# Ordering TensorE's work by tile shape, with two PSUM banks instead of three for transposes and attention outputs

## The chip, the cores and the metric

The kernel runs on one core of a Trainium2 chip. The metric is device time in microseconds (us) for one execution. The kernel before was run three times: 494.48, 492.61 and 491.35 us, median 492.61. One execution was also profiled, and all rows in this document come from such profiles. Engines are named as in the profile: PE is TensorE, DVE is VectorE, ACT is ScalarE, POOL is GpSimd, SP issues DMAs.

## The reference

Two stages over 8 batches of 576 positions. Stage 1 is window attention with 8 heads of 64 columns; its output, heads side by side, is the input x of stage 2, a mixture of four attention experts of which each position uses two.

```python
# stage 1, per batch and head
scores = (q @ k.T) / 8;  mask = (0 <= row - col < 64)
attn = softmax(where(mask, scores, -1e9));  y = attn @ v
# stage 2, per batch, x is (576, 512)
logits = x @ w_gate                  # 4 experts, the 2 largest are kept, softmax over them gives w
for e in range(4):
    q, k, v = x @ wq[e], x @ wk[e], x @ wv[e]
    a = softmax(causal(q @ k.T / 8))
    out += (e is chosen) * w[e] * (a @ v @ wo[e])
```

## The kernel before

**Stage 1** works in 36 units of eight (head pair, 64-row block) pieces. `s1_qk` multiplies queries by two key blocks each into two PSUM banks of the tag `s`; ACT and DVE gather the wanted half into `sm`, and the softmax follows: maximum (DVE), subtraction (POOL), exponential (ACT), sum and reciprocal (DVE), scaling (POOL). In the first five units (`u < EARLY`) the subtraction is instead the bias of eight ACT exponentials of 64 columns. `s1_t` transposes the result on PE into one bank of the tag `t`; ACT copies it (`ft`), DVE multiplies it twice by a mask straight out of the bank (`pt<-t,tri`), POOL masks the other half out of `ft`. `s1_av` multiplies by v into another `t` bank, and ACT and DVE split the result into a high and a low float32r part (`xh`, `xl`).

**Stage 2** works by batch and by pair of experts (`pr`). `s2_v`, `s2_k`, `s2_q` project x with three products each (high times high, high times low, low times high) into `s` banks. `s2_mm` makes the scores in four blocks k, two `s` banks each, and `s2_soft` their softmax in place in the tiles `p` (maxima on DVE, exponentials on ACT, and `s2_w` scales by the gate on POOL). `s2_t` transposes them into `t` banks (tiles `t2_b_pr_part_k`), ACT copies them to `pt`, `s2_av_mm` multiplies by v (`o2_b_pr_part`, tag `t`), and `s2_av_out` splits that into `yh` and `yl`. `s2_o` is the output projection: six products of 512 columns into an `s` bank (`ops`), a copy on DVE into `out`, and a DMA.

**PSUM** has eight banks: five for the tag `s`, three for `t`.

**The order** is made by the class `Plan`. Each call is only recorded, with a position `at` on a scale where one half step n is one expert pair of one batch; `Plan.order` then plays the recorded instructions on five engines with assumed lengths (`length`), assumed time to hop between engines, an assumed cost for PE when the tile shape changes (`SWITCH`), and the number of buffers per tag. Whenever an engine is free it takes the ready instruction with the lowest `place`. The result is the fixed program order of each engine. The tile shape (`mode`) of a PE instruction is the pair of rows and columns of the array that it uses: 128x128 for transposes and all projections, 64x128 for the scores of stage 2, 64x64 for the scores of stage 1, 128x64 for the products with v. All instructions of the profile carry line 241, where the recorded calls are made, so they are told apart by tile names.

Of the kernel before, what the change touches and what calls it, by code (L numbers as in the profile page):

```python
# [29 lines left out]
CPOS = 0.202  # L30
EARLY = 5
AFFINITY = 0.0
UNFOLD = (2, 2)
BPOS = ((0.044, 0.7), (0.088, 0.667), (0.08, 0.3, 0.12), (-0.413, -0.1))
# [4 lines left out]
class Plan:  # L39
# [3 lines left out]
    OVERLAP = {"V": 85, "A": 105, "G": 30, "P": 0, "S": 0}  # L43
    SWITCH = 105
    HOP = 40
# [189 lines left out]
    def place(self, op, mode):  # L235
        return op["at"] - (AFFINITY if op["mode"] == mode is not None else 0)

# [19 lines left out]
def window_attention_moe_attention(ctx: ExitStack, tc: tile.TileContext, qT, kT, vW,  # L257
# [105 lines left out]
    def s1_qk(u):  # L363

        banks = [psum.tile([128, 4, 128], F32, tag="s", bufs=5, name=f"s1_{u}_{x}") for x in range(2)]
        with nc.block():
# [36 lines left out]
    def s1_t(u):  # L403

        ps = psum.tile([128, 4, 128], F32, tag="t", bufs=3, name=f"t1_{u}")
        sm = SM.pop(u).rearrange("r x j c -> r (x j c)")
        with nc.block():
            for i in range(4):
                nc.tensor.transpose(ps[:, i], sm[:, 128 * i:128 * i + 128], ident)
        t = PT1[u] = work.tile([128, 4, 2, 128], F32, tag="pt1", bufs=2, name=f"pt1_{u}")  # L410
        f = work.tile([128, 4, 128], F32, tag="ft", bufs=1, name=f"ft_{u}")
        nc.scalar.activation(f, ps, AF.Copy)
        for e in range(2):
            r = slice(64 * e, 64 * e + 64)
            if e < UNFOLD[u >= EARLY]:
                nc.vector.tensor_mul(t[0:64, :, e], ps[r],
                                     tri[r].rearrange("r a c -> r (a c)")[:, None, :].to_broadcast([64, 4, 128]))
            for half in range(e < UNFOLD[u >= EARLY], 2):
                nc.gpsimd.affine_select(out=t[64 * half:64 * half + 64, :, e].rearrange("r i (a c) -> r i a c", a=2),
                                        in_=f[r].rearrange("r i (a c) -> r i a c", a=2), pattern=[[0, 4], [0, 2], [2 * half - 1, 64]],  # L420
                                        base=half - 1, channel_multiplier=1 - 2 * half, compare_op=OP.is_ge, fill=0.0)

    freed = []

    def s1_av(u):
        t = PT1.pop(u)
        o = psum.tile([128, 8, 64], F32, tag="t", bufs=3, name=f"o1_{u}")
        with nc.block():
# [100 lines left out]
    def s2_v(b, j):  # L529


        ps = psum.tile([128, 512], F32, tag="s", bufs=5, name=f"v2ps_{b}_{j}")
        with nc.block():
# [56 lines left out]
    def proj(b, name, pr, half):  # L590
        c0, n = HALVES[b > 0][half]
        ps = psum.tile([128, 512], F32, tag="s", bufs=5, name=f"{name}ps_{b}_{pr}_{half}")
        w = slice(128 * pr, 128 * pr + 128)
# [38 lines left out]
    def s2_mm(b, pr, k):  # L632
        banks = SB[b, pr, k] = [psum.tile([128, 512], F32, tag="s", bufs=5, name=f"s2_{b}_{pr}_{k}_{e}")
                                for e in range(2)]
# [53 lines left out]
    def s2_w(b, pr, k):  # L688
# [7 lines left out]
        for x in range(x0, x1):  # L696
            i, e = (x + 1) // 2, (x + 1) % 2
            p = PX[0][:, 0] if x == 0 else P2S[pr][i > 2][:, row(i, e):row(i, e) + 64 + 128 * i]
            nc.gpsimd.tensor_scalar(p, p, r2[:, 3, x:x + 1], 1.0, op0=OP.mult, op1=OP.mult)

    def s2_t(b, pr, part, k):
        ps = psum.tile([128, 512], F32, tag="t", bufs=3, name=f"t2_{b}_{pr}_{part}_{k}")
        pt = PT2[part]
# [43 lines left out]
        else:  # L747
# [18 lines left out]
    def s2_av_mm(b, pr, part):  # L766
        b0, b1 = PARTS[part]
        n = 64 * (b1 - b0)
        o = OB[b, pr, part] = psum.tile([128, 512], F32, tag="t", bufs=3, name=f"o2_{b}_{pr}_{part}")
        with nc.block():  # L770
# [5 lines left out]
    def s2_av_out(b, pr, part):  # L776
        b0, b1 = PARTS[part]
        o = OB.pop((b, pr, part))
        for x0, x1 in ([(b0, b1)] if b % 2 == 0 or b1 < BLK else [(b0, b1 - 1), (b1 - 1, b1)]):
            src = o[:, 64 * (x0 - b0):64 * (x1 - b0)]  # L780
            y0 = y_col(b, x0)
            yh, yl = (y[pr][:, y0:y0 + 64 * (x1 - x0)] for y in (YH, YL))
            nc.scalar.activation(yh, src, AF.Copy)
            nc.vector.tensor_sub(yl, src, yh)

    def s2_o(b, j):
        ps = psum.tile([128, DM], F32, tag="s", bufs=5, name=f"ops_{b}_{j}")
# [14 lines left out]
    def half(n):  # L802
# [10 lines left out]
        if 0 <= zb < NB and n >= 2:  # L813
# [120 lines left out]
```

## Time and profile before

| | |
|---|---|
| median of three runs | 492.61 us (491.35 to 494.48) |
| profiled execution | 494.5 us, span of its instructions 492.8 us |
| PE busy | 466.4 us, 95% of the span |
| DVE, ACT, POOL busy | 356.0, 309.5, 231.5 us (72%, 63%, 47%) |
| mean granted clock of PE | 0.985 |
| HBM | 39.85 MB read, 9.44 MB written |

How to read it: a PE row's duration runs from its start to a modelled end, and the next matmul starts before that end. So the difference between the starts of two rows is the better measure of what a block of matmuls takes on PE. Idle time of an engine is given with what released it.

### The profile page before, as it was taken

The numbers are of one execution on the slowest core, as the hardware profiler recorded it, in microseconds if no ns is written. First come the engines' busy times: TensorE is split into PE (matmuls) and PEld (weight loads), VectorE is DVE, ScalarE is ACT, GpSimd is POOL, SyncE is SP. The second block draws the span as 40 slices with busy tenths as digits, with TensorE's granted clock in tenths as the row PEclk, the third lists the DMA queues.
The fourth block names the chain that finished last, engine by engine and source line by source line (L and its number), as shares of the span: only waits on it lengthen the run. The fifth ranks groups of instructions, "written<-read, shape, count | busy, mean of one in ns | idle before, by whom it ended". The sixth has DMA issues, their size and how long they took to land.

```text
span 492.8 us, 14724 instructions
## 1 busy us (share of the span) xinstructions
PE 466.4 (95%) x5672; PEld 411.8 (84%) x5672; DVE 356.0 (72%) x1186; ACT 309.5 (63%) x967; POOL 231.5 (47%) x434
## 2 busy tenths in 40 slices
PE   5597979999999999999999999999999999999986
PEld 3487968898889988898889988898888988898774
DVE  4778987988777967687776868868776875555712
ACT  4566556767575766757567676667567575656751
POOL 3456647563555464562555544462555450512130
PEclk9979989999999999999999999999999999999989
DMA  7954742214362323223451324234120011001103
GB/s 232 386 180 152 235 145 68 81 49 120 122 187 86 107 88 99 75 94 98 140 189 51 103 86 136 77 98 125 66 92 1 2 45 40 27 1 45 43 2 108
DMA packets 21782, 50.24 MB, mean 102 GB/s; under 512 B 2896, under 2 KB 5456, under 8 KB 21712
## 3 DMA queue, kind: packets, MB, share of 16 engines
q1 hardware_dynamic: 21712, 49.30, 30.7%
q8 instruction: 45, 0.74, 0.6%
q14 instruction: 25, 0.20, 0.1%
HBM read 39.85 MB, written 9.44 MB: 100 GB/s over the span
## 4 chain that ended last, share of the span: by engine, by line
PE 86%; DVE 6%; ACT 4%; issue 1%; POOL 1%; DMA 1%; SPq 1%; POOLq 0%; ACTq 0%
PE s L241 17%; PE o L241 17%; PE t L241 13%; PE ops L241 11%; PE qps L241 10%; PE v2ps L241 10%; PE kps L241 10%; ACT sm L241 2%; DVE st L241 2%; DVE pt L241 2%; DMA k<-in_kT_dram 1%; DVE sm L241 1%; ACT p L241 1%; SPq L241 1%; DVE p L241 0%
## 5 line engine op out<-in xcount | busy, mean ns | idle before, releaser
L241 POOL TENSOR_TENSOR sm<-sm,st 128x512 f32<-128x512 f32 x67 | 71.5, 1070 | 86.4 <-DVE st L241 53.6
L241 PE MATMUL o<-pt,v 128*64 128x64 f32 (+3 forms) x2048 | 94.3, 248 | 6.7 <-DVE pt L241 3.5
L241 PEld LDWEIGHTS o<-pt,v 128*64 128x64 f32 x2048 | 84.8, 142 | 17.3 <-issue 8.3
L241 POOL TENSOR_SCALAR p<-p,r 128x192 f32<-128x192 f32 (+3 forms) x128 | 72.7, 587 | 38.7 <-DVE r L241 24.0
L241 ACT ACTIVATE p<-p,r 128x192 f32<-128x192 f32 (+3 forms) x128 | 77.6, 608 | 21.2 <-DVE r L241 21.0
L241 ACT ACTIVATE pt<-t 128x512 f32<-128x512 f32 (+2 forms) x192 | 69.8, 386 | 15.9 <-PE t L241 13.8
L241 DVE CUSTOM_DVE_ANT_0 p<-s,causal 128x320 f32<-128x320 f32 (+3 forms) x160 | 70.5, 471 | 11.5 <-PE s L241 10.3
L241 POOL TENSOR_SCALAR_AFFINE_SELECT pt<-ft 64x512 f32<-64x512 f32 x72 | 48.3, 671 | 54.8 <-ACT ft L241 50.7
L241 PE MATMUL t<-ident,p 128*128 128x128 f32 x384 | 58.5, 278 | 1.0 <-POOL p L241 0.8
L241 DVE TENSOR_REDUCE st<-sm 128x8 f32<-128x512 f32 x72 | 49.0, 681 | 9.0 <-ACT sm L241 8.1
L241 DVE TENSOR_TENSOR pt<-t,tri 64x512 f32<-64x512 f32 x72 | 49.4, 686 | 6.4 <-ACT ft L241 5.3
L241 PE MATMUL s<-kt,qt 64*128 64x256 f32 (+2 forms) x480 | 53.2, 336 | 0.4 <-DVE logits L241 0.4
L241 PEld LDWEIGHTS t<-ident,p 128*128 128x128 f32 x384 | 43.5, 142 | 9.8 <-issue 4.0
L241 PE MATMUL s<-k,q 64*64 64x128 f32 (+1 forms) x1152 | 45.4, 293 | 6.2 <-DMA k<-in_kT_dram 4.6
L241 PEld LDWEIGHTS s<-k,q 64*64 64x64 f32 x1152 | 35.5, 147 | 12.9 <-issue 4.7
L241 PEld LDWEIGHTS s<-kt,qt 64*128 64x128 f32 x480 | 34.9, 186 | 10.6 <-issue 4.1
L241 DVE COPY_PREDICATED sm<-own,s 128x256 f32<-128x256 uint8 x72 | 30.9, 444 | 14.2 <-ACT sm L241 9.7
L241 PE MATMUL qps<-xh,wqhi 128*128 128x320 f32 (+1 forms) x128 | 40.5, 316 | 0.1
L241 PE MATMUL kps<-xh,wkhi 128*128 128x320 f32 (+1 forms) x128 | 39.5, 309 | 0.0
L241 PE MATMUL v2ps<-wvhi,xh 128*128 128x260 f32 x128 | 38.7, 303 | 0.0
L241 PE MATMUL qps<-xl,wqhi 128*128 128x320 f32 (+1 forms) x128 | 37.6, 294 | 0.0
L241 PE MATMUL kps<-xh,wklo 128*128 128x320 f32 (+1 forms) x128 | 37.6, 294 | 0.0
(106 smaller groups left out, 1028.7 us busy)
## 6 DMA issues: line engine op xcount, KB each, us to landing
v<-in_vW_dram SPq DMA_DIRECT2D x32, 576.0 KB, 4.0
out_dram<-out SPq DMA_DIRECT2D x32, 256.0 KB, 2.0
q<-in_qT_dram SPq DMA_DIRECT2D x28, 288.0 KB, 3.2
k<-in_kT_dram SPq DMA_DIRECT2D x28, 288.0 KB, 4.1
out_dram<-out SPq DMA_DIRECT2D x8, 128.0 KB, 2.3
q<-in_qT_dram SPq DMA_DIRECT2D x4, 160.0 KB, 5.5
k<-in_kT_dram SPq DMA_DIRECT2D x4, 160.0 KB, 4.9
q<-in_qT_dram SPq DMA_DIRECT2D x4, 128.0 KB, 2.3
```

The costliest lines, as they stand in the source:

```text
L241: call(*args, **kw)
```

## The change

- `AFFINITY` goes from 0 to 0.6: `place` lets an instruction of PE's present tile shape come up to 0.6 of a half step before its position. It holds for positions below 15 (`2 * NB - 1`).
- `SWITCH` and several assumed lengths in `length` change (transposes, float32 and float32r products, POOL and ACT instructions).
- The tag `s` has six banks and `t` two. The transposes of the last batch take `s` banks.
- `EARLY` is gone: all 36 units subtract on POOL and use one exponential of 512 columns. `UNFOLD`, which was (2, 2), is gone; what it selected stays.
- The four output projections of batch 6 get one position, `OLATE` = 1.7 half steps after the start of their half step. So that they can still read the values of batch 6, those of batch 7 (and the last block of batch 6, which is projected with it) are put in buffers of their own, taken from the tags `xh` and `xl`.
- In the last batch the copies of the second and fourth output projection are made on ACT.

```diff
+OLATE = 1.7
+TTAG = 1
+AFFINITY = 0.6
-EARLY = 5
-AFFINITY = 0.0
-UNFOLD = (2, 2)
...
-    SWITCH = 105
+    SWITCH = 100
...
         if name == "transpose":
-            return 109
+            return 105
         if ins[0].dtype == F32R:
-            return (0.215 * n + 13) if rows == 64 else max(109, 0.43 * n + 10)
+            return (0.215 * n + 19) if rows == 64 else 0.43 * n + 14
         if rows == 64:
-            return max(28, 0.43 * n)
-        return 2 * max(28, 0.43 * n) if cols == 64 else 2 * max(110, 0.86 * n)
+            return 33 + 0.22 * n
+        return 6 + 0.86 * n if cols == 64 else 20 + 1.72 * n
...
     def place(self, op, mode):
-        return op["at"] - (AFFINITY if op["mode"] == mode is not None else 0)
+        return op["at"] - (AFFINITY if op["mode"] == mode and op["at"] < 2 * NB - 1 else 0)
...
-        if u < EARLY:
-            nc.vector.tensor_scalar(st[:, 0], st[:, 0], 0.125, None, op0=OP.mult)
-            for i in range(8):
-                nc.scalar.activation(flat[:, i], flat[:, i], AF.Exp, bias=st[:, 0, i:i + 1], scale=0.125)
-        else:
-            nc.gpsimd.tensor_tensor(flat, flat, st[:, 0, :, None].to_broadcast([128, 8, 64]), op=OP.add)
-            nc.scalar.activation(flat, flat, AF.Exp, scale=0.125)
+        nc.gpsimd.tensor_tensor(flat, flat, st[:, 0, :, None].to_broadcast([128, 8, 64]), op=OP.add)
+        nc.scalar.activation(flat, flat, AF.Exp, scale=0.125)
...
-        ps = psum.tile([128, 4, 128], F32, tag="t", bufs=3, name=f"t1_{u}")
+        ps = psum.tile([128, 4, 128], F32, tag="t", bufs=2, name=f"t1_{u}")
...
+    T2 = (dict(tag="t", bufs=2), dict(tag="s", bufs=6))
+
     def s2_t(b, pr, part, k):
-        ps = psum.tile([128, 512], F32, tag="t", bufs=3, name=f"t2_{b}_{pr}_{part}_{k}")
+        ps = psum.tile([128, 512], F32, **T2[b == NB - 1 and TTAG], name=f"t2_{b}_{pr}_{part}_{k}")
...
+    def y_buf(b, blk):
+
+        if b < NB - 2 or b == NB - 2 and blk < BLK - 1:
+            return YH, YL
+        if not Y7:
+            for x in ("xh", "xl"):
+                t = work.tile([128, NP * S], F32R, tag=x, name=f"y7{x}")
+                Y7.append([t[:, 1152 * i:1152 * i + S + 64] for i in range(2)])
+        return Y7
...
-        nc.vector.tensor_copy(t, ps)
+        if b == NB - 1 and j % 2:
+            nc.scalar.activation(t, ps, AF.Copy)
+        else:
+            nc.vector.tensor_copy(t, ps)
...
             if zp == 1:
-                spread("O0", [(s2_o, zb, j) for j in range(2)])
-                spread("O1", [(s2_o, zb, j) for j in range(2, 4 + zb % 2)])
+                if zb == NB - 2:
+                    it += [(n + OLATE, s2_o, (zb, j)) for j in range(4)]
+                else:
+                    spread("O0", [(s2_o, zb, j) for j in range(2)])
+                    spread("O1", [(s2_o, zb, j) for j in range(2, 4 + zb % 2)])
```

What this does to PE's program order, counted over its 4056 matmuls: the tile shape changes 236 times before and 157 times with the change. By the shape that is entered: 64x128 63 times before and 41 now, 128x64 51 and 45, 64x64 32 and 19, 128x128 90 and 52. From the first score block of batch 1 to that of batch 7 the counts are 167 and 91. The matmuls themselves are the same.

Three places in the order, PE alone. The first is in the middle, where batch 3 ends and batch 4 begins, from the same transpose on. Only the first row or rows of each block are shown; names are tile, then unit or batch, pair and block. Before:

```order
L241 MATMUL t2_3_1_1_2_721<-ident_86,p2_2_69 128x128 x4
L241 MATMUL s1_27_0_725<-k24_612,q24_611 64x64 x2
...
L241 MATMUL t2_3_1_1_3_722<-ident_86,p2_2_69 128x128 x4
L241 MATMUL kps_4_1_1_729<-xh4_517,wkhi_171 128x256
...
L241 MATMUL o1_26_733<-pt1_26_716,v23_620 64x64 x16
L241 MATMUL o2_3_1_1_735<-pt2_1_88,v2_1_102 64x64 x2
...
L241 MATMUL s2_4_0_2_0_736<-kt_4_0_682,qt0_91 128x320
...
L241 MATMUL s1_28_0_740<-k24_612,q24_611 64x128 x2
...
L241 MATMUL s2_4_0_3_0_738<-kt_4_0_682,qt0_91 128x256
...
L241 MATMUL t1_27_730<-ident_86,sm1_27_727 128x128 x4
```

With the change:

```order
L241 MATMUL t2_3_1_1_2_721<-ident_86,p2_2_69 128x128 x4
L241 MATMUL s1_27_0_725<-k24_612,q24_611 64x64 x2
...
L241 MATMUL s1_28_0_740<-k24_612,q24_611 64x128 x2
...
L241 MATMUL t2_3_1_1_3_722<-ident_86,p2_2_69 128x128 x4
L241 MATMUL t2_4_0_0_0_747<-ident_86,p2_0_67 128x128 x4
L241 MATMUL s2_4_0_3_0_738<-kt_4_0_682,qt0_91 128x256
...
L241 MATMUL s2_4_1_2_0_797<-kt_4_1_703,qt1_92 128x320
...
L241 MATMUL o1_26_733<-pt1_26_716,v23_620 64x64 x16
L241 MATMUL o2_3_1_1_735<-pt2_1_88,v2_1_102 64x64 x2
...
L241 MATMUL s1_29_0_777<-k25_641,q25_640 64x128 x2
...
L241 MATMUL t2_4_0_0_1_758<-ident_86,p2_0_67 128x128 x4
```

Two units of 64x64 now stand together, then two transposes, then two score blocks, then the products with v as before. In the first piece the shape changes seven times over ten blocks (a projection `kps` among them), in the second six times over eleven.

The second place is a little earlier, with the change alone. The built program puts `t1_26` and `o2_3_1_0` in the same one of the two `t` banks, so `o2_3_1_0` waits until ACT and DVE have read `t1_26`:

```order
L241 MATMUL t1_26_715<-ident_86,sm1_26_695 128x128 x4
L241 MATMUL o1_25_704<-pt1_25_684,v22_614 64x64 x14
L241 MATMUL o1_25_704<-pt1_25_684,v23_620 64x64 x2
L241 MATMUL s2_4_0_1_0_709<-kt_4_0_682,qt0_91 128x448
...
L241 MATMUL s2_4_0_2_0_736<-kt_4_0_682,qt0_91 128x320
...
L241 MATMUL o2_3_1_0_706<-pt2_0_87,v2_1_102 64x64 x2
```

Between the two stand 16 products with v and two score blocks of six.

The third is in the last batch, from the last small score product on. Before:

```order
L241 MATMUL s2_7_1_1_0_1053<-kf_7_1_1018,qf1_98 128x64
L241 MATMUL t2_7_0_1_0_1061<-ident_86,p2_1_68 128x128 x4
L241 MATMUL s2_7_1_2_0_1062<-kt_7_1_1019,qt1_92 128x320
...
L241 MATMUL s2_7_1_3_0_1064<-kt_7_1_1019,qt1_92 128x256
...
L241 MATMUL t2_7_0_1_2_1058<-ident_86,p2_1_68 128x128 x4
L241 MATMUL t2_7_1_0_2_1059<-ident_86,px_70 128x128
L241 MATMUL t2_7_0_1_1_1060<-ident_86,p2_1_68 128x128 x4
L241 MATMUL t2_7_1_0_1_1066<-ident_86,p2_0_67 128x128 x4
L241 MATMUL o2_7_0_1_1068<-pt2_1_88,v2_1_102 64x64 x2
...
L241 MATMUL t2_7_1_0_0_1067<-ident_86,p2_0_67 128x128 x4
L241 MATMUL t2_7_1_1_0_1070<-ident_86,p2_2_69 128x128 x4
```

With the change:

```order
L241 MATMUL s2_7_1_1_0_1047<-kf_7_1_1020,qf1_98 128x64
L241 MATMUL t2_7_0_1_0_1055<-ident_86,p2_1_68 128x128 x4
L241 MATMUL s2_7_1_3_0_1058<-kt_7_1_1021,qt1_92 128x256
...
L241 MATMUL ops_6_2_1070<-wohi_237,yh0_93 128x512
...
L241 MATMUL ops_6_3_1072<-wohi_237,yh0_93 128x512
...
L241 MATMUL t2_7_1_0_2_1053<-ident_86,px_70 128x128
L241 MATMUL t2_7_0_1_1_1054<-ident_86,p2_1_68 128x128 x4
L241 MATMUL t2_7_1_0_1_1060<-ident_86,p2_0_67 128x128 x4
L241 MATMUL o2_7_0_1_1062<-pt2_1_88,v2_1_102 64x64 x2
...
L241 MATMUL t2_7_1_0_0_1061<-ident_86,p2_0_67 128x128 x4
L241 MATMUL t2_7_1_1_0_1064<-ident_86,p2_2_69 128x128 x4
```

Two output projections of batch 6 now stand between the last scores and the transpose of `px`, and the score block k = 2 (`s2_7_1_2`) has gone ahead, out of this piece. In DVE's order the copies of these two projections stand between the two groups of gate scales (`r`) of the last pair.

## Rows read from the trace of the kernel before

**Rows 1.** Page, the chain that ended last: shares by engine, by tile.

```profile
PE 86%; DVE 6%; ACT 4%; issue 1%; POOL 1%; DMA 1%; SPq 1%; POOLq 0%; ACTq 0%
PE s L241 17%; PE o L241 17%; PE t L241 13%; PE ops L241 11%; PE qps L241 10%; PE v2ps L241 10%; PE kps L241 10%; ACT sm L241 2%; DVE st L241 2%; DVE pt L241 2%; DMA k<-in_kT_dram 1%; DVE sm L241 1%; ACT p L241 1%; SPq L241 1%; DVE p L241 0%
```

**Rows 2.** Busy time by stretch.

```profile
core 0: us, PE busy (x) PEld busy (x) DVE busy (x) ACT busy (x) POOL busy (x), PEclk, DMA share, GB/s
0.00:100.00 100.00, 81.35 (x1132) 70.89 (x1133) 78.91 (x235) 60.69 (x190) 56.40 (x126) 0.95 0.55 183
...
112.00:442.00 330.00, 329.62 (x4021) 293.38 (x4019) 244.97 (x845) 215.00 (x673) 158.86 (x282) 1.00 0.28 88
...
460.00:480.00 20.00, 17.33 (x161) 14.02 (x161) 8.52 (x38) 14.02 (x44) 6.31 (x11) 0.91 0.07 27
```

**Rows 3.** PE timeline: start us, duration us, engine, line, operation, tiles, shapes, count.

```profile
203.60 1.09 PE L241 MATMUL t<-ident,p 128*128 128x128 f32 x8
...
206.51 0.70 PE L241 MATMUL s<-kt,qt 64*128 64x320 f32 x6
207.15 1.09 PE L241 MATMUL s<-k,q 64*64 64x128 f32 x32
208.17 0.66 PE L241 MATMUL t<-ident,p 128*128 128x128 f32 x4
208.75 0.62 PE L241 MATMUL s<-kt,qt 64*128 64x256 f32 x6
209.30 1.15 PE L241 MATMUL o<-pt,v 128*64 128x64 f32 x32
```

**Rows 4.** PE timeline: two score blocks joined, and what follows.

```profile
461.54 1.07 PE L241 MATMUL s<-kt,qt 64*128 64x256 f32 x12
462.54 1.21 PE L241 MATMUL o<-pt,v 128*64 128x64 f32 x20
```

**Rows 5.** PE timeline: a projection between two score blocks, its first three matmuls.

```profile
255.81 0.39 PE L241 MATMUL v2ps<-wvhi,xh 128*128 128x260 f32 x1
256.04 0.28 PE L241 MATMUL v2ps<-wvlo,xh 128*128 128x260 f32 x1
256.16 0.29 PE L241 MATMUL v2ps<-wvhi,xl 128*128 128x260 f32 x1
...
257.46 0.47 PE L241 MATMUL s<-kt,qt 64*128 64x448 f32 x2
```

**Rows 6.** ACT and DVE groups that read a stage-1 transpose: count, busy us, mean ns.

```profile
L241 ACT ACTIVATE ft<-t 128x512 f32<-128x512 f32 x36 | 21.3, 592 | 3.0 <-PE t L241 2.5
...
L241 DVE TENSOR_TENSOR pt<-t,tri 64x512 f32<-64x512 f32 x72 | 49.4, 686 | 6.4 <-ACT ft L241 5.3
```

**Rows 7.** Timelines of PE and DVE: one stage-1 transpose, and its last readers.

```profile
247.58 0.66 PE L241 MATMUL t<-ident,sm 128*128 128x128 f32 x4
...
250.39 1.40 DVE L241 TENSOR_TENSOR pt<-t,tri 64x512 f32<-64x512 f32 x2
```

**Rows 8.** PE timeline after the last scores.

```profile
468.97 0.33 PE L241 MATMUL t<-ident,px 128*128 128x128 f32 x1 [1.64 <-POOL px L241]
...
471.31 3.60 PE L241 MATMUL o<-pt,v 128*64 128x64 f32 x36
474.85 0.34 PE L241 MATMUL t<-ident,p 128*128 128x128 f32 x1
```

**Rows 9.** PE timeline: the same product with v, the last of the kernel.

```profile
481.74 1.98 PE L241 MATMUL o<-pt,v 128*64 128x64 f32 x36
```

**Rows 10.** POOL timeline after the last scores.

```profile
468.95 3.06 POOL L241 TENSOR_SCALAR p<-p,r 128x192 f32<-128x192 f32 x6
472.18 1.46 POOL L241 TENSOR_SCALAR p<-p,r 128x576 f32<-128x576 f32 x2 [0.17 <-DVE r L241]
```

**Rows 11.** ACT and POOL groups of the stage-1 subtraction: count, busy us, mean ns.

```profile
L241 ACT ACTIVATE sm<-sm,st 128x64 f32<-128x64 f32 x40 | 10.2, 335 | 4.5 <-DVE st L241 4.5
...
L241 POOL TENSOR_TENSOR sm<-sm,st 128x512 f32<-128x512 f32 x67 | 71.5, 1070 | 86.4 <-DVE st L241 53.6 <-ACT pt L241 7.4 <-ACT xh L241 4.9
```

More of the change, by code (lines that the diff above doesn't have):

```diff
@@ L76, in length @@
         if engine == "A":
-            return (165 if psum else 205) + 0.83 * n + (230 if len(outs) > 1 else 0)
+            return (165 if psum else 205) + 0.83 * n + (230 if len(outs) > 1 else 75 if len(ins) > 1 else 0)
         if engine == "V":
             n = max([n] + [x.free_size() for x in ins])
-            return 152 + 1.04 * n + (65 if len(outs) > 1 else 0)
+            return 152 + 1.04 * n
         if engine == "G":
             return {"tensor_tensor": 60 + 1.97 * n, "affine_select": 190 + 0.94 * n,
-                    "memset": 100 + 0.8 * n}.get(name, 265 + 0.85 * n)
+                    "memset": 100 + 0.7 * n}.get(name, (265 if outs[0].shape[0] > 64 else 190) + 0.83 * n)
         if engine == "S":
@@ L363, in s1_qk @@
     def s1_qk(u):
-        banks = [psum.tile([128, 4, 128], F32, tag="s", bufs=5, name=f"s1_{u}_{x}") for x in range(2)]
+        banks = [psum.tile([128, 4, 128], F32, tag="s", bufs=6, name=f"s1_{u}_{x}") for x in range(2)]
         with nc.block():
@@ L414, in s1_t @@
             r = slice(64 * e, 64 * e + 64)
[L415 to L421, printed above, removed]
+            nc.vector.tensor_mul(t[0:64, :, e], ps[r],
+                                 tri[r].rearrange("r a c -> r (a c)")[:, None, :].to_broadcast([64, 4, 128]))
+            nc.gpsimd.affine_select(out=t[64:128, :, e].rearrange("r i (a c) -> r i a c", a=2),
+                                    in_=f[r].rearrange("r i (a c) -> r i a c", a=2), pattern=[[0, 4], [0, 2], [1, 64]],
+                                    base=0, channel_multiplier=-1, compare_op=OP.is_ge, fill=0.0)
     freed = []
@@ L426, in s1_av @@
         t = PT1.pop(u)
-        o = psum.tile([128, 8, 64], F32, tag="t", bufs=3, name=f"o1_{u}")
+        o = psum.tile([128, 8, 64], F32, tag="t", bufs=2, name=f"o1_{u}")
         with nc.block():
@@ L529, in s2_v @@
     def s2_v(b, j):
-        ps = psum.tile([128, 512], F32, tag="s", bufs=5, name=f"v2ps_{b}_{j}")
+        ps = psum.tile([128, 512], F32, tag="s", bufs=6, name=f"v2ps_{b}_{j}")
         with nc.block():
@@ L591, in proj @@
         c0, n = HALVES[b > 0][half]
-        ps = psum.tile([128, 512], F32, tag="s", bufs=5, name=f"{name}ps_{b}_{pr}_{half}")
+        ps = psum.tile([128, 512], F32, tag="s", bufs=6, name=f"{name}ps_{b}_{pr}_{half}")
         w = slice(128 * pr, 128 * pr + 128)
@@ L632, in s2_mm @@
     def s2_mm(b, pr, k):
-        banks = SB[b, pr, k] = [psum.tile([128, 512], F32, tag="s", bufs=5, name=f"s2_{b}_{pr}_{k}_{e}")
+        banks = SB[b, pr, k] = [psum.tile([128, 512], F32, tag="s", bufs=6, name=f"s2_{b}_{pr}_{k}_{e}")
                                 for e in range(2)]
@@ L754, in s2_t @@
             odd(256, 768)
+    Y7 = []
+    def y_buf(b, blk):
[6 more added lines that the diff above has]
+        return Y7
     def y_col(b, blk):
@@ L768, in s2_av_mm @@
         n = 64 * (b1 - b0)
-        o = OB[b, pr, part] = psum.tile([128, 512], F32, tag="t", bufs=3, name=f"o2_{b}_{pr}_{part}")
+        o = OB[b, pr, part] = psum.tile([128, 512], F32, tag="t", bufs=2, name=f"o2_{b}_{pr}_{part}")
         with nc.block():
@@ L778, in s2_av_out @@
         o = OB.pop((b, pr, part))
-        for x0, x1 in ([(b0, b1)] if b % 2 == 0 or b1 < BLK else [(b0, b1 - 1), (b1 - 1, b1)]):
+        for x0, x1 in ([(b0, b1)] if (b % 2 == 0 and b < NB - 2) or b1 < BLK else [(b0, b1 - 1), (b1 - 1, b1)]):
             src = o[:, 64 * (x0 - b0):64 * (x1 - b0)]
             y0 = y_col(b, x0)
-            yh, yl = (y[pr][:, y0:y0 + 64 * (x1 - x0)] for y in (YH, YL))
+            yh, yl = (y[pr][:, y0:y0 + 64 * (x1 - x0)] for y in y_buf(b, x0))
             nc.scalar.activation(yh, src, AF.Copy)
@@ L786, in s2_o @@
     def s2_o(b, j):
-        ps = psum.tile([128, DM], F32, tag="s", bufs=5, name=f"ops_{b}_{j}")
+        ps = psum.tile([128, DM], F32, tag="s", bufs=6, name=f"ops_{b}_{j}")
         with nc.block():
@@ L790, in s2_o @@
                 y0 = y_col(b, 2 * j) if j < 4 else 512
-                yh, yl = (y[pr][:, y0:y0 + 128] for y in (YH, YL))
+                yh, yl = (y[pr][:, y0:y0 + 128] for y in y_buf(b, 2 * j))
                 three(ps, yh, yl, whi["o"][:, pr], wlo["o"][:, pr], pr == 0, pr == 1)
```

## The prediction

> **What bounds the kernel now.** I read the page's chain of waits first. It is 86% TensorE, spread over scores, products with v, transposes and projections [rows 1], so no single wait sets the end; the sum of TensorE's work does. The busy time by stretch says where that holds [rows 2]: from 112 to 442 us PE is busy for 329.62 of 330 us at a granted clock of 1.00, while DVE, the next busiest, has 244.97. What PE saves there comes off the end one for one, until DVE binds. In the first 100 us PE is idle for 100 - 81.35 = 18.7 us; between 460 and 480 for 2.7, with the clock at 0.91.
>
> The timeline of PE then shows what the order itself costs. Start-to-start times are used, since durations overlap.
> - Two score blocks that stand apart between other shapes take 206.51 to 207.15 = 0.64 and 208.75 to 209.30 = 0.55 [rows 3], 1.19 together. Joined, six of 256 and six of 320 columns take 461.54 to 462.54 = 1.00 [rows 4]. One visit to the shape, entry and exit together, costs 0.19 us.
> - Transposes: eight last 1.09 and four 0.66 [rows 3], so four more take 0.43. Four between other shapes take 208.17 to 208.75 = 0.58: 0.15 for the visit.
> - Projections: of twelve matmuls between two score blocks the first step is 0.23, the next 0.12, the whole 255.81 to 257.46 = 1.65 [rows 5], against 12 x 0.12 = 1.44: 0.21, half of it (0.11) at entry and half (0.10) at exit.
>
> **The change part by part.** *Fewer changes of shape.* In the program orders 236 changes become 157, 79 fewer, 76 of them between the first scores of batch 1 and of batch 7, the stretch where PE never waits. By visits: 64x128 22 fewer x 0.19 = 4.2; 128x128 38 fewer x 0.17 (between transposes' 0.15 and projections' 0.21, since most visits hold both) = 6.5; 64x64 13 fewer and 128x64 6 fewer. For the last two no row separates a visit; the bounds are 0.10 (an exit alone) and 0.21, and I take 0.15, the value of the transposes, which like them are plain float32: 2.0 and 0.9. Sum **-13.5 us**; ends 79 x 0.10 = -7.9 and 79 x 0.21 = -16.6.
>
> The Trainium skill, TensorEngine Tiling (Array Packing), section Tiling Modes, says that changing the tiling mode, and not merely the tile, drains TensorE. If the drain at the exit were all, this term would be -7.9 instead of -13.5. The rows agree that a change costs, and show as much again at the entry [rows 5].
>
> *Two t banks instead of three.* This is the wait that is added. A stage-1 transpose's bank is read by an ACT copy (0.592) and two DVE products (0.686 each) [rows 6], 1.97 us if nothing is queued before them. In one unit the transposes start at 247.58 and last 0.66, and the second DVE product ends at 250.39 + 1.40 = 251.79 [rows 7]: 3.5 us after the last transpose. In the order with the change, at its tightest in the middle (`t1_26` to `o2_3_1_0`), there lie a unit's products with v (1.15 [rows 3]) and two joined score blocks (1.0 to 1.2 [rows 3, 4]) between the transposes and the next writer of that bank, 2.3 us. So a stage-1 unit waits between 0 and 1.2 us there; behind the waiting matmul stands all of PE. I take the low end: the planner that counts banks left 0.4 us of idle time in 330 [rows 2], it now counts two, and most units have more room. 0.07 us for each of 36 units: **+2.5**, ends 0 and +8. The sixth `s` bank can only loosen; its term is in the same range.
>
> *The end.* The last pair's softmax leaves PE idle, 1.64 us before `px` and 1 us after it (2.67 in all) [rows 2, 8]. Two projections of batch 6 now stand there. One costs 11% of 492.8 over 36 [rows 1] = 1.5 us, so they fill 3.0; the PE work itself only moves, from a stretch with no pause. I take **-2.0**, ends 0 and -2.7: the scaling on POOL still takes 3.06 + 1.46 one after the other [rows 10], so part of the pause may come back before the second part's transposes. The copies of the two projections stand in DVE's order before the last `r`; two of about 0.69 (the DVE row of 512 columns [rows 6]) end while POOL is in its 3.06, so I cost them at nothing; if POOL were done sooner, up to 0.7 would show. The four output DMAs go later on SP, behind all loads; nothing waits for them but the end, and batch 7's come after.
>
> *The clock at the end.* After these pauses the product with v took 3.60 us, the same 36 rows at the end 1.98 [rows 8, 9]; the granted clock of that stretch is 0.91, half speed for a part of it [rows 2]. With the pauses filled I take **-1.6**; ends 0 and -1.6.
>
> *The first five units.* Eight ACT exponentials, 10.2/5 = 2.0 us per unit, become one of 512 columns (nearest the copy's 0.59 [rows 6]) and a POOL subtraction of 1.07 [rows 11], about 0.4 less in the chain of each unit. POOL has room (56.40 of 100 [rows 2]). But five chains overlap, `t` has a bank less, and the order of the units shifts: **-0.5**, ends -4 and +4.
>
> *Nothing* is taken for the copies on ACT in the last batch, the buffers for batch 7 (the last copy and DMA stay), the moved loads (DMA share 0.28 [rows 2]), and the changed lengths, which act through the order alone.
>
> Sum: -13.5 + 2.5 - 2.0 - 1.6 - 0.5 = **-15.1 us**. The profiled execution took 494.5, so it would take 479.4. It was the slowest of the three shown; the median is 1.9 lower, which gives 477.5. I predict **478 us** as the median, the forecast's own range 473 to 483.
>
> **The rivals.**
> 1. *The waits take half of it.* Units wait 0.3 us each on `t` banks (36 x 0.3 = 11 instead of 2.5): 486. For it: a bank is now written anew every 2 x 480/202 = 4.8 us, by 202 tiles on two banks, where 216 on three had 6.8 us, and [rows 7] is slower than the room. Against: the reader that was late there was late because nobody needed the bank.
> 2. *The exit alone costs*: -7.9 instead of -13.5: 483.
> 3. *Slower.* The third `t` bank was what covered the readers. Each of the 36 units waits 0.7 us, half-way to the 1.2 of the tightest place and 0.1 beyond, 25 us instead of 2.5: 500. It takes back the gain from (15.1 + 2.5)/36 = 0.49 us a unit on. Such pauses would also cost clock, as those at 469 did. Against it stands that 1.97 us of reading fits in 2.3.
> 4. *No change*: the same waits at 0.35 to 0.5 us, or DVE as the bound. DVE's 244.97 in a stretch of 317 us says no to the second as an average; only its bursts could.
>
> One page names rival 3's clock: the Trainium skill, TensorE: Matmul & The Clock Gate, section "A second HAM failure mode: psum-queue depth-cycling", where PE idles briefly between groups as it goes through banks, and its clock swings. In this trace three banks kept 1.00 for 330 us. With the 0.91 of the end's pauses in that stretch, (330 - 13.5) x (1/0.91 - 1) = 31 us would be added: 509.
>
> **How the numbers follow.** Forecast 0.68, rival 1 0.12, rival 2 0.08, no change 0.07, slower 0.05 (the clock's case 0.02 of it). A measurement of this kernel tells about 1% from no change, 487.7 to 497.5. Faster: 0.68 + 0.12 + 0.08 = 0.88; within 1% 0.07; slower 0.05. The range takes in the forecast but for its lowest end, and rivals 1 and 2: 474 to 487, leaving out 0.12 above and about 0.05 below.
>
> **What would show it.** PE's starts: more rows of x12 scores and x64 stage-1 scores, each visit 0.15 to 0.2 cheaper; the first scores of batch 7 some 11 us earlier than 442. Idle time of PE between 112 and 430 us with ACT or DVE readers of `t` or `o` as releasers would show rival 1 or 3; joined blocks that take as long as separate ones, rival 2. Before `px` no pause, and the product after it near 2 us; if it again takes 3.6, the clock's term is wrong. The forecast fails if PE's idle time in the middle exceeds some 8 us, or if the first 100 us grow by more than 4.

## The result, and the profile after

The changed kernel takes **469.74 us** (median of four runs, 468.92 to 470.31) against 493.38 for the kernel before (median of four, the three runs above and one of 494.15): ratio 0.9524, 95% interval 0.9487 to 0.9561. The prediction was 478.0 with a range of 474 to 487. The direction was right; the time came out 8.3 us below the forecast and below its range. Single executions of 732 us (b_aff), 882 us (b_banks62) and 1103 us (the kernel before) are left out of all ratios, and the profile of b_aff, which is of the first, is not used.

The profiled execution took 470.31 us, its span is 468.5. The page's chain of the changed kernel, shares by engine and by tile:

```profile
PE 76%; DVE 12%; ACT 4%; POOL 3%; issue 2%; DMA 1%; SPq 1%; POOLq 0%; DVEq 0%
PE o L241 14%; PE s L241 12%; PE t L241 12%; PE v2ps L241 11%; PE ops L241 10%; PE kps L241 9%; PE qps L241 8%; DVE st L241 3%; DVE pt L241 2%; ACT p L241 2%; DVE p L241 2%; POOL p L241 1%; DVE sm L241 1%; POOL sm L241 1%; ACT sm L241 1%
```

Against [rows 1] DVE has doubled its share, from 6% to 12%. Busy time by stretch, changed kernel. The second stretch runs from the score block k = 0 of batch 1 (106.80) to that of batch 7 (423.14); one other block of batch 1 already stands at 97.20, joined to the last of batch 0. The third stretch is the last pair's softmax:

```profile
core 0: us, PE busy (x) PEld busy (x) DVE busy (x) ACT busy (x) POOL busy (x), PEclk, DMA share, GB/s
0.00:100.00 100.00, 88.06 (x1220) 78.05 (x1221) 85.11 (x244) 58.27 (x166) 64.57 (x136) 0.93 0.57 188
107.00:423.00 316.00, 314.71 (x4024) 290.56 (x4022) 244.35 (x836) 213.26 (x669) 156.63 (x280) 1.00 0.28 92
442.00:460.00 18.00, 17.82 (x182) 14.70 (x181) 7.39 (x27) 12.66 (x39) 4.79 (x9) 1.00 0.16 60
```

Read them against [rows 2]. In the first 100 us PE is idle for 11.9 us, where it was 18.7. The middle has shrunk from 330 to 316 us and is as full as before, with 1.3 us of idle time and the clock at 1.00. At the end the clock is 1.00 too, where it was 0.91.

PE's timeline at the end, changed kernel (start us, duration us, engine, line, operation, tiles, shapes, count, idle time before and its releaser):

```profile
438.56 1.09 PE L241 MATMUL t<-ident,p 128*128 128x128 f32 x8
439.58 1.06 PE L241 MATMUL s<-kt,qt 64*128 64x256 f32 x12
440.57 0.33 PE L241 MATMUL t<-ident,px 128*128 128x128 f32 x1
...
447.49 0.27 PE L241 MATMUL t<-ident,px 128*128 128x128 f32 x1
447.60 0.90 PE L241 MATMUL t<-ident,p 128*128 128x128 f32 x5
448.67 0.55 PE L241 MATMUL t<-ident,p 128*128 128x128 f32 x3 [0.18 <-POOL p L241]
449.15 1.98 PE L241 MATMUL o<-pt,v 128*64 128x64 f32 x36
```

Eight transposes and twelve scores now run in one piece each. The `px` of the last pair (447.49) has no pause before it, 0.18 us is all that is left of 2.67, and the product of 36 rows takes 1.98 us, as in [rows 9], not the 3.60 of [rows 8].

What the two profiled executions differ by, 24.3 us of span, falls to these parts. The price of a change of shape is the one measured below.

| | predicted, us | measured, us | from |
|---|---|---|---|
| 79 fewer changes of shape | -13.5 | -12.9 | 79 x 0.163 (a_aff0; interval 0.12 to 0.21) |
| PE idle before batch 1's k = 0 scores | -0.5 | -6.7 | 18.65 to 11.94 |
| PE idle in the middle | +2.5 | +0.9 | 0.37 to 1.29 |
| PE idle from batch 7's k = 0 scores on, up to PE's last matmul | -2.0 | -2.5 | 2.67 to 0.18 |
| product of 36 at half clock | -1.6 | -1.6 | 3.60 to 1.98 |
| sum | -15.1 | -22.8 | 1.5 of the 24.3 stay unassigned |

So 6.2 of the 7.7 us between the two sums lie in one row, the front of the program. This row is known to about 2 us: b_o6late has PE's order of the kernel before, and a_o6spread that of the change, for all but the last batch (3803 and 3811 of the 4056 matmuls), and there PE is idle for 16.93 and 12.52 us. In time, batch 1's k = 0 scores begin 5.7 us earlier (112.49 to 106.80; in the other pair 112.16 to 106.28, 5.9 earlier). Seven of the 79 changes of shape lie before them, 1.1 us, so 4.6 to 4.8 us of the front are something else.

### The profile page after: what moved, and what is told of

It reads as the page before. It is cut to its first block, busy times and chain, and to the rows that moved or that the text cites. A ratio compares the mean times of both kernels' runs of the same rounds, so it can differ in the third digit from the quotient of the medians.

```text
span 468.5 us, 14682 instructions
## 1 busy us (share of the span) xinstructions
PE 450.4 (96%) x5672; PEld 408.4 (87%) x5672; DVE 356.0 (76%) x1181; ACT 304.3 (65%) x936; POOL 235.8 (50%) x439
## 4 chain that ended last, share of the span: by engine, by line
PE 76%; DVE 12%; ACT 4%; POOL 3%; issue 2%; DMA 1%; SPq 1%; POOLq 0%; DVEq 0%
PE o L241 14%; PE s L241 12%; PE t L241 12%; PE v2ps L241 11%; PE ops L241 10%; PE kps L241 9%; PE qps L241 8%; DVE st L241 3%; DVE pt L241 2%; ACT p L241 2%; DVE p L241 2%; POOL p L241 1%; DVE sm L241 1%; POOL sm L241 1%; ACT sm L241 1%
## 5 line engine op out<-in xcount | busy, mean ns | idle before, releaser
L241 POOL TENSOR_TENSOR sm<-sm,st 128x512 f32<-128x512 f32 x72 | 75.7, 1055 | 76.3 <-DVE st L241 58.1
L241 PEld LDWEIGHTS o<-pt,v 128*64 128x64 f32 x2048 | 82.7, 141 | 11.6 <-issue 7.2
L241 PE MATMUL o<-pt,v 128*64 128x64 f32 (+3 forms) x2048 | 90.7, 246 | 1.9 <-DVE pt L241 1.1
L241 ACT ACTIVATE pt<-t 128x512 f32<-128x512 f32 (+3 forms) x192 | 71.0, 386 | 15.5 <-PE t L241 12.7
L241 DVE CUSTOM_DVE_ANT_0 p<-s,causal 128x320 f32<-128x320 f32 (+3 forms) x160 | 69.0, 469 | 9.5 <-PE s L241 9.0
L241 PE MATMUL t<-ident,p 128*128 128x128 f32 x384 | 57.5, 275 | 0.5 <-POOL p L241 0.2
L241 PE MATMUL s<-kt,qt 64*128 64x256 f32 (+2 forms) x480 | 46.9, 324 | 0.6 <-DVE r L241 0.5
L241 PE MATMUL s<-k,q 64*64 64x128 f32 (+1 forms) x1152 | 41.5, 287 | 5.8 <-DMA k<-in_kT_dram 5.5
L241 POOL TENSOR_SCALAR px<-px,r 128x64 f32<-128x64 f32 x16 | 5.1, 317 | 65.9 <-DVE r L241 45.5
L241 PE MATMUL kps<-xl,wkhi 128*128 128x320 f32 (+1 forms) x128 | 37.7, 294 | 0.0
```

The costliest lines, as they stand in the source:

```text
L241: call(*args, **kw)
```

## Where the front lost its pauses

PE's waits in the first 112 us, kernel before (who waited for whom: us in total, times, longest us):

```profile
PE s L241 <- DMA k<-in_kT_dram: 4.6, 3, 3.6
PE o L241 <- DVE pt L241: 3.5, 5, 1.0
PE t L241 <- POOL sm L241: 3.4, 2, 2.4
PE o L241 <- POOL pt L241: 3.2, 2, 1.6
PE t L241 <- DVE st L241: 2.1, 1, 2.1
```

And of the changed kernel:

```profile
PE s L241 <- DMA k<-in_kT_dram: 5.5, 4, 3.5
PE t L241 <- POOL sm L241: 3.3, 2, 2.3
PE o L241 <- DVE pt L241: 0.9, 1, 0.9
PE o L241 <- POOL pt L241: 0.7, 1, 0.7
```

The waits for loads stayed. Those of the transposes for the softmax (`sm`, `st`) went from 5.5 to 3.3 us, and the smaller rows that are not shown come to 1.5 both times. Most of what went is the wait of the products with v for `pt`: 3.5 + 3.2 = 6.7 us became 1.6 (2.4 in a_o6spread, the same order at another clock). `pt` is the masked transpose, so the chain is transpose, copy on ACT, products on DVE and masking on POOL, product with v. PE's timeline shows what stands in that chain's time. Before:

```profile
13.30 1.11 PE L241 MATMUL t<-ident,sm 128*128 128x128 f32 x4 [2.14 <-DVE st L241]
16.00 0.70 PE L241 MATMUL o<-pt,v 128*64 128x64 f32 x8 [1.58 <-POOL pt L241]
17.46 1.55 PE L241 MATMUL o<-pt,v 128*64 128x64 f32 x24 [0.76 <-DVE pt L241]
18.93 1.99 PE L241 MATMUL s<-k,q 64*64 64x128 f32 x32
```

Changed kernel:

```profile
13.63 0.65 PE L241 MATMUL t<-ident,sm 128*128 128x128 f32 x4 [2.30 <-POOL sm L241]
14.21 0.45 PE L241 MATMUL s<-k,q 64*64 64x128 f32 x8
15.73 1.67 PE L241 MATMUL s<-k,q 64*64 64x128 f32 x24 [1.06 <-DMA k<-in_kT_dram]
17.33 1.97 PE L241 MATMUL o<-pt,v 128*64 128x64 f32 x32
```

Before, nothing stood between the transpose and its product, and PE waited 1.58 + 0.76 us. Now the scores of unit 3 stand there. They start 4.7 us earlier than they did (14.21 against 18.93) and fill time in which PE has nothing else, though 24 of their 32 matmuls now wait 1.06 us for a load. Which part of the change made this order is what half of the experiments ask.

## The experiments

All runs were timed against the kernel before on the same chip. Differences against the kernel before are (ratio - 1) x 494 us, those against the changed kernel (ratio - 0.9524) x 494. Taken from the intervals of the ratios, the first are known to about 1 to 1.5 us either way (b_aff to 3), the second to about 2 to 3.5.

**Shapes.** The change without the preference for the present shape, and the kernel before with it alone:

```diff
-AFFINITY = 0.6
+AFFINITY = 0.0
```

> The changed kernel with AFFINITY = 0 and all else kept; its order has 237 shape changes where the changed kernel has 157 (the middle 170 against 91). Theory S (a change of shape costs PE 0.15 to 0.2 us, entry and exit): 80 more x 0.17 = 13.6, so about 483. Rival E (only the exit, 0.10): 478. Rival O (the gain is from waits, banks and lengths, not from the shapes): within 3 us of 469.7.

Ratio 0.9789 (0.9728 to 0.9851): 13.1 us slower than the change, for 80 changes: 0.163 us each, with an interval of 0.12 to 0.21. It is still 10.4 us faster than the kernel before, with one change of shape more.

```diff
-        return op["at"] - (AFFINITY if op["mode"] == mode is not None else 0)
+        return op["at"] - (AFFINITY if op["mode"] == mode and op["at"] < 2 * NB - 1 else 0)
-AFFINITY = 0.0
+AFFINITY = 0.6
```

> The kernel before with AFFINITY = 0.6 (for positions below 15) and nothing else; 166 shape changes against 236, three t banks and five s banks as before. Theory S: 70 fewer x 0.17 = 11.9, about 481.5. Rival E: 486.5. Rival O: within 3 us of 493.4. PE idle time in the middle within 2 us of before's 0.4.

Ratio 0.9756 (0.9692 to 0.9820): 12.1 us for 70 changes, 0.172 each, with an interval of 0.13 to 0.22. Taken away or added, the price agrees, and so does the term of the prediction: theory S holds, and the 0.10 of rival E lies outside both intervals. What b_aff was to show of PE's idle time in the middle is not shown. The other 10 us of the change are not shapes.

**Early units.** All units subtract on POOL, alone on the kernel before; and the old early units within the change:

```diff
-EARLY = 5
+EARLY = 0
```

> The kernel before with all units subtracting on POOL and one exponential (EARLY = 0), nothing else; 237 shape changes. Theory F1: 488 to 489. Rival F2: 492 to 494.5.

Ratio 0.9934 (0.9910 to 0.9958), 3.3 us faster. The median, 490.5 us, lies between what the two theories gave, so neither holds as it stands. In its first 112 us the products wait 3.0 us for `pt` (2.0 for DVE, 1.0 for POOL) instead of 6.7. The scores of unit 3 stand before the first product here too, and that product no longer waits for `pt`:

```profile
14.48 0.71 PE L241 MATMUL s<-k,q 64*64 64x128 f32 x8
...
17.93 1.97 PE L241 MATMUL o<-pt,v 128*64 128x64 f32 x32
```

```diff
+        if u < 5:
+            nc.vector.tensor_scalar(st[:, 0], st[:, 0], 0.125, None, op0=OP.mult)
+            for i in range(8):
+                nc.scalar.activation(flat[:, i], flat[:, i], AF.Exp, bias=st[:, 0, i:i + 1], scale=0.125)
+        else:
...
```

> The changed kernel with the first five stage-1 units as before (eight ACT exponentials of 64 columns with bias instead of a POOL subtraction and one exponential of 512). Theory F1 (the shorter softmax of these units is what made the first 112 us 5.7 us shorter): 474 to 475. Rival F2 (the order of PE in the first 112 us, which fills pauses with the next unit's scores, made it): 469 to 471, of which 1.2 us are its 7 more shape changes.

Ratio 0.9537 (0.9495 to 0.9579): 0.6 us slower than the change, less than its seven changes of shape cost, near rival F2 and outside F1. The early units seem to be worth less within the change than alone, but the interval, 2.8 us either way, still reaches the 3.3. In that profile PE is idle 3.0 us longer (16.45 against 13.41) and the clock never falls, so how much of the one hid the other is open.

**Assumed lengths.** The whole of `length` and `SWITCH` of the change put into the kernel before (b_newlen), the part on PE alone (b_newlen_pe), the part on DVE, ACT and POOL alone (b_newlen_rest), and the old ones put back into the change (a_oldlen). The edits are those of the diff ahead; the part on DVE, ACT and POOL is shown here. It brings the assumed lengths nearer to the rows of the kernel before: an ACT exponential of 64 columns with bias takes 335 ns [rows 11], where the old length gave 258 and the new one gives 333; a DVE reduction over 320 columns of scores (`p<-s,causal`) 484 (old 550, new 485); a POOL instruction on 64 x 128 elements (`v<-vo`) 297 (old 374, new 296).

```diff
-            return (165 if psum else 205) + 0.83 * n + (230 if len(outs) > 1 else 0)
+            return (165 if psum else 205) + 0.83 * n + (230 if len(outs) > 1 else 75 if len(ins) > 1 else 0)
-            return 152 + 1.04 * n + (65 if len(outs) > 1 else 0)
+            return 152 + 1.04 * n
-                    "memset": 100 + 0.8 * n}.get(name, 265 + 0.85 * n)
+                    "memset": 100 + 0.7 * n}.get(name, (265 if outs[0].shape[0] > 64 else 190) + 0.83 * n)
```

> Before, with only the assumed lengths of the change. 240 changes of shape instead of 236, +0.6 us. Theory L (better lengths make a better order, and that is a good part of the 11 us that are not shapes): 3 to 5 us faster than before, with less idle time of PE in the first 112 us. Rival (they act only together with the rest): within 1 us.

Ratio 0.9940 (0.9911 to 0.9970), 3.0 us faster, at four changes of shape more: the low end of theory L. PE is idle 13.3 us before batch 1's scores instead of 18.65.

> Before, with the assumed lengths of TensorE and SWITCH of the change, those of DVE, ACT and POOL as before. 236 changes of shape, as before. If TensorE's lengths made the better front: 2.5 to 3.5 us faster than before, idle time before batch 1 near 13 us instead of 18. If the lengths of the other engines did: within 1 us of before, idle time near 18.

Ratio 0.9978 (0.9958 to 0.9998), 1.1 us faster: at the edge of what the second case allowed, and far from the first. PE is idle for 16.5 us before batch 1's scores, not near 18. Its waits in the first 112 us:

```profile
PE o L241 <- POOL pt L241: 5.7, 6, 1.5
PE s L241 <- DMA k<-in_kT_dram: 4.9, 4, 3.5
PE o L241 <- DVE pt L241: 3.6, 4, 1.2
```

> Before, with the assumed lengths of DVE, ACT and POOL of the change, those of TensorE and SWITCH as before. 241 changes of shape, +0.8 us. If these lengths carry the better front: 2 to 3 us faster than before, idle time before batch 1 near 13.5 us instead of 17 to 18.6. Rival (only both kinds together do it): within 1 us.

Ratio 0.9949 (0.9923 to 0.9975), 2.5 us faster, with five changes more. The time is as expected; the idle time was 15.3 us, not 13.5. Its waits in the same stretch:

```profile
PE s L241 <- DMA k<-in_kT_dram: 4.4, 3, 3.5
PE t L241 <- POOL sm L241: 3.0, 2, 1.7
PE qps L241 <- DVE m L241: 2.0, 1, 2.0
PE t L241 <- DVE sm L241: 1.5, 1, 1.5
PE o L241 <- POOL pt L241: 1.5, 1, 1.5
```

With PE's lengths alone the products wait 9.3 us for `pt`, with those of the other engines alone 1.5. The waits separate the two; the times, 1.1 and 2.5 us, have intervals that overlap. The place is another than the one shown above. PE's timeline in b_newlen_rest:

```profile
15.84 2.28 PE L241 MATMUL o<-pt,v 128*64 128x64 f32 x32 [1.48 <-POOL pt L241]
...
25.00 1.65 PE L241 MATMUL s<-k,q 64*64 64x128 f32 x32
26.57 1.15 PE L241 MATMUL o<-pt,v 128*64 128x64 f32 x32
```

The first product still waits, as before: the scores that stand ahead of it in the change are the work of the early units (b_early0 and a_oldlen have them there, b_newlen, b_newlen_rest and a_early5 do not). The lengths of DVE, ACT and POOL put the scores of unit 4 ahead of unit 2's product, which waited 0.98 us before and does not now; with PE's lengths alone these scores stay behind it, and it waits 1.23. Unit 1's product does not wait either (1.64 and 0.58 us before), but the transposes ahead of it now wait 1.71 us for the softmax on POOL, so not all of it is won. That the planner does so because it now reckons the chain on these engines to end at another time is argued from its code and not measured.

> The change, with the old assumed lengths. 166 changes instead of 157, +1.4 us. Theory L: 4 to 6 us slower than the change, the idle time of PE in the first 112 us back. Rival (AFFINITY and the early units carry the front): 1 to 2 us slower, no more than the nine changes cost.

Ratio 0.9628 (0.9580 to 0.9677): 5.1 us slower than the change, of which nine changes of shape are 1.5. PE is idle 15.7 us before batch 1's scores against 11.9, not the whole 18.65. In the first 112 us it waits 2.8 us for `pt`, against 1.6, and 2.7 us for the gate scales `r`, against 0.5. The lengths are worth some 3 us alone and 5 within the change, the latter known to 3 us either way.

**The banks.** Six and two on the kernel before, for every tile of the two tags; the same with the last batch's transposes in `s` banks; five and three in the change. The first:

```diff
-        ps = psum.tile([128, 4, 128], F32, tag="t", bufs=3, name=f"t1_{u}")
+        ps = psum.tile([128, 4, 128], F32, tag="t", bufs=2, name=f"t1_{u}")
...
```

> Before, with six s banks and two t banks and nothing else. 231 changes instead of 236, -0.8 us. Theory B (the sixth s bank lets the projections and scores of the first 112 us run ahead): 2 to 4 us faster, with less idle time there. Rival W (two t banks make PE wait, as the prediction had it): 1 to 3 us slower, with idle time of PE in the middle released by readers of t or o.

Ratio 1.0057 (1.0035 to 1.0078), 2.8 us slower. Rival W had the size right and the place wrong: in the middle PE does not wait at all. PE's timeline at its end:

```profile
468.45 0.33 PE L241 MATMUL t<-ident,px 128*128 128x128 f32 x1 [2.06 <-ACT pt L241]
...
470.02 1.97 PE L241 MATMUL t<-ident,p 128*128 128x128 f32 x8 [0.81 <-ACT pt L241]
...
475.79 0.63 PE L241 MATMUL t<-ident,p 128*128 128x128 f32 x4 [0.78 <-ACT yh L241]
...
482.45 2.27 PE L241 MATMUL o<-pt,v 128*64 128x64 f32 x36 [0.63 <-ACT pt L241]
```

Most of these waits are for ACT to read a bank (`pt`, `yh`); the kernel before waits there for POOL above all [rows 8].

```diff
-        ps = psum.tile([128, 512], F32, tag="t", bufs=2, name=f"t2_{b}_{pr}_{part}_{k}")
+        ps = psum.tile([128, 512], F32, name=f"t2_{b}_{pr}_{part}_{k}",
+                       **(dict(tag="t", bufs=2), dict(tag="s", bufs=6))[b == NB - 1])
```

> Before, with six s and two t banks, and the last batch's transposes in s banks as in the change. If the loss of 2.8 us with two t banks alone was made in the last batch: 2 to 3 us faster than that, the same as before within 1 us, the pauses of the tail back to 3 us. Rival (it was made elsewhere, by an order that fits worse): still 2 to 3 us slower than before.

Ratio 1.0004 (0.9985 to 1.0023): the loss is gone, and so are the waits for ACT at the end. From batch 7's k = 0 scores to the end of the program the profiles have 50.8 us before, 52.7 with two `t` banks throughout and 50.7 here. The change's use of `s` banks in the last batch pays for the missing `t` bank; the cost that the runs can tell lay in the last batch, where little other work is left.

```diff
-        banks = [psum.tile([128, 4, 128], F32, tag="s", bufs=6, name=f"s1_{u}_{x}") for x in range(2)]
+        banks = [psum.tile([128, 4, 128], F32, tag="s", bufs=5, name=f"s1_{u}_{x}") for x in range(2)]
...
```

> The change, with five s and three t banks. 173 changes of shape instead of 157, +2.5 us. Theory W (two t banks cost PE 2.8 us, as alone on the kernel before): within 0.5 us of the change, idle time down by 2 to 3 us. Rival (in the new order two t banks cost next to nothing): 2 to 3 us slower, idle time the same within 1 us.

Ratio 0.9603 (0.9561 to 0.9645): 3.9 us slower, 2.6 of it by 16 changes of shape; idle time 14.3 us against 13.4. Theory W falls and the rival holds, with a loss above its 2 to 3 us but within the interval (2.8 us either way): in the new order the sixth `s` bank is worth more than the third `t` bank. It does not do so by joining score blocks: of the 16 changes only one enters 64x128 (42 against 41), 11 enter 128x128 (63 against 52) and 4 enter 128x64.

**The late projections.** Alone on the kernel before (with their buffers and the copies on ACT), and taken out of the change:

```diff
+                if zb == NB - 2:
+                    it += [(n + OLATE, s2_o, (zb, j)) for j in range(4)]
+                else:
...
```

> Before, with only the late projections of batch 6, the buffers of their own and the copies on ACT. Theory T (they fill the pauses of the last pair and keep the clock): 3 to 4 us faster, no pause over 0.5 us before px, the product of 36 that follows near 2 us instead of 3.6. Rival (the pauses come back after it, or the clock falls all the same): 0 to 1.5 us faster.

Ratio 0.9930 (0.9906 to 0.9953), 3.5 us faster. PE's timeline:

```profile
464.41 0.33 PE L241 MATMUL t<-ident,px 128*128 128x128 f32 x1
...
465.77 0.33 PE L241 MATMUL t<-ident,p 128*128 128x128 f32 x1 [0.60 <-POOL p L241]
466.28 0.55 PE L241 MATMUL t<-ident,p 128*128 128x128 f32 x3 [0.18 <-POOL p L241]
...
468.59 2.97 PE L241 MATMUL o<-pt,v 128*64 128x64 f32 x56
```

Of the pauses of [rows 8] 0.78 us is left, and the product keeps its clock: 56 rows, 36 and 20 joined, in 2.97 us.

```diff
-                if zb == NB - 2:
+                if False:
```

> The change, with the projections of batch 6 spread as before. 156 changes of shape. Theory T (late projections fill the last pair's pauses and keep the clock, 3.5 us alone on the kernel before): 3 to 4 us slower than the change, pauses of 2 us and more around px. Rival (in the new order something else fills them): 0 to 1 us slower.

Ratio 0.9614 (0.9568 to 0.9660), 4.4 us slower than the change. The pause is back, and the clock falls behind it, to 0.72 between 449 and 455 us:

```profile
449.65 0.33 PE L241 MATMUL t<-ident,px 128*128 128x128 f32 x1 [3.31 <-POOL px L241]
...
452.29 2.80 PE L241 MATMUL o<-pt,v 128*64 128x64 f32 x36
```

Theory T holds both ways, at 3.5 and 4.4 us: the prediction's two terms for the end made 3.6.

**Can it be better?** Three variants of the change: `AFFINITY` 0.7, and `SWITCH`, the planner's price of a change of shape, at 170 and 190 ns, near the 163 to 172 measured.

```diff
-AFFINITY = 0.6
+AFFINITY = 0.7
```

> The change, with AFFINITY 0.7. 150 changes of shape instead of 157. Theory S (0.155 us a change, and nothing else moves): 1.1 us faster than the change, ratio to the kernel before 0.950. Rival (steps pulled further ahead make others late): same or up to 2 us slower, with 1 to 3 us more idle time of PE.

Ratio 0.9578 (0.9540 to 0.9617), 2.7 us slower (2.6 either way) with seven changes fewer. Idle time rose by 2.3 us, which is the rival.

```diff
-    SWITCH = 100
+    SWITCH = 170
```

> The change, with 170 instead of 100 ns assumed for a change of shape. 149 changes of shape instead of 157, -1.4 us. Theory (assumed costs that fit the chip leave less idle time): 2 to 5 us faster than the change. Rival (the steps are only shuffled): within 1 us, or slower by idle time that comes back.

Ratio 0.9529 (0.9504 to 0.9554): the same as the change. Idle time is 15.6 us against 13.4, which takes back the eight changes' 1.3 us.

```diff
-    SWITCH = 100
+    SWITCH = 190
```

> The same with 190 ns. 151 changes of shape, -1.1 us. Theory: 2 to 6 us faster than the change. Rival: within 1 us, or slower.

Ratio 0.9559 (0.9535 to 0.9583), 1.7 us slower, within the noise of 2.2 us either way; PE is idle 5.4 us between batch 1's and batch 7's scores, where the change has 1.3. The theory that an assumed cost nearer to the measured one must give a better order falls here: it did for the lengths of DVE, ACT and POOL and did not for the price of a change. No version beat the change.

## Why the prediction was right and wrong

**What bounds it: right.** PE's work sets the end in the middle, and what PE saves there came off.

**Shapes: right**, -13.5 predicted, -12.9 by the measured price. The prediction weighed the drain alone, 0.10 us a change and -7.9 in all, against entry and exit together, 0.17. Both runs on `AFFINITY` give 0.163 to 0.172, and both intervals start above 0.10. With 0.10 for the exit from [rows 5] some 0.07 is left for the entry, between 0.02 and 0.12; the exit by itself would have left 5 us of each run unexplained. Rival 2 falls. The Trainium skill, TensorEngine Tiling (Array Packing), section Tiling Modes, names the drain and gives no price.

**Two t banks: the wait was sized too high and looked for in the wrong place.** PE's idle time in the middle rose by 0.9 us, not 2.5, of which at most 0.2 us can be a wait for such a bank, released by the DVE products that read one. The bank's price lies in the last batch (b_banks62), and the change avoids it there (b_banks62_ttag), a part of the diff that the prediction did not cost at all. Taken together the sixth `s` bank and the missing `t` bank cost nothing alone (+0.2 us) and gain within the change (3.9 us, 2.6 of them through shapes, a_banks53), where the prediction added 2.5. Rivals 1 and 3 fall: 36 units that each wait 0.3 or 0.7 us are not there. The granted clock of the middle is 1.00 with two banks as with three. The Trainium skill, TensorE: Matmul & The Clock Gate, section "A second HAM failure mode: psum-queue depth-cycling", describes a clock that swings while PE, cycling through banks, idles briefly between groups; this trace does not show it.

**The end: right**, -2.0 and -1.6 predicted, -2.5 and -1.6 in the profile, 3.5 to 4.4 us by the two runs.

**The first five units: the step that failed.** The prediction took -0.5 us for them, between -4 and +4, and *nothing* for the changed lengths, "which act through the order alone". The idle time there fell by 6.7 us (by 4.4 in the other pair of profiles), and the front became 4.6 to 4.8 us shorter by other things than shapes: beyond the end of the range. Of the 8.3 us by which the forecast was off, this is the largest part. The early units are worth 3.3 us alone (b_early0); the lengths, costed at nothing, are worth 2.5 to 3.0 alone and about 5 within the change (b_newlen_rest, b_newlen, a_oldlen). The prediction reckoned how much shorter one unit's chain becomes. For the first unit it did not become shorter: its transposes start at 13.30 us before, at 13.44 with the early units alone and at 13.63 with the change. What counted there was what PE does during the chain; for the other units the two are not separated. The profile of before had it: 6.7 of the 18.65 us of idle time were products waiting for `pt`. The prediction used the 18.7 of [rows 2] and not the waits behind them, and it looked at three places of the order, none of them in the first 30 us.

The whole in one line: -3.3, -3.0, -3.5, +0.2 and -12.1 us, the five parts alone on the kernel before (early units, lengths, late projections, banks with the last batch's transposes, preference), sum to -21.7, known to about 4 us; the change gave -23.6. That the parts add up so nearly is in part luck; the banks, for one, are not worth the same alone (+0.2) and within the change (-3.9).

## What to carry to other kernels

Where a planner writes the order, its assumed lengths are part of the kernel: corrected lengths on engines with time to spare (DVE, ACT, POOL) moved TensorE's work into its own pauses. Before costing a change at nothing because it only reorders, list who TensorE waits for in each stretch and read the new order at those places. Idle time of one profile is a rough measure (two profiles of one order differed by 1.7 us); the start of a named block is a better one. A buffer taken away costs where no other work is left, so look at the last stage first. A cost that is closer to the chip is no guarantee of a better order; count changes of shape and idle time together, and time it.

## What the runs showed of the hardware

The clock at the start is not set by the order alone. The change and a_o6spread have the same first 3811 matmuls in PE's order, up to the last batch. Busy time by stretch, changed kernel:

```profile
10.00:20.00 10.00, 6.60 (x86) 5.17 (x84) 8.62 (x20) 3.77 (x8) 7.02 (x8) 0.74 1.01 359
20.00:30.00 10.00, 8.84 (x116) 7.59 (x115) 8.81 (x15) 6.15 (x12) 5.09 (x13) 0.57 0.76 274
```

a_o6spread:

```profile
10.00:20.00 10.00, 6.47 (x97) 4.65 (x89) 8.84 (x21) 4.26 (x9) 7.08 (x8) 1.00 1.00 362
20.00:30.00 10.00, 8.44 (x135) 7.57 (x136) 9.55 (x17) 7.31 (x16) 7.20 (x17) 1.00 0.96 347
...
60.00:70.00 10.00, 8.51 (x116) 7.08 (x120) 9.35 (x37) 6.13 (x19) 4.58 (x9) 0.74 0.36 109
70.00:80.00 10.00, 10.00 (x90) 9.31 (x83) 6.43 (x22) 7.31 (x25) 6.67 (x14) 0.92 0.35 128
```

From 10 to 30 us the granted clock was 0.74 and 0.57 in the one execution and 1.00 in the other. The first projection of batch 0 came at 28.80 and 26.28 us, 2.5 us apart, and the distance stayed at 2.3 to 2.5 us until 68 us. By 73 us it had fallen to 0.5, and batch 1's k = 0 scores came at 106.80 and 106.28. No pause of PE gave the time back: between 60 and 80 us it was a_o6spread's clock that fell, to 0.74 and 0.92, while the changed kernel had 1.00. Each execution lost some 2 us to its clock once, in another place. At the end of the program the clock cost 1.6 us before and nothing with the change.
